# Loading w_in's v columns in pieces of 128 columns, with a lower limit on what is queued ahead of a transfer

## The chip, the core and the metric

The kernel runs on one core of a Trainium2 chip. The metric is the device time of one execution in microseconds, the median of several runs; lower is better.

## The reference

Attention over 8 heads is followed by a gated feed-forward block with a mixing over the sequence. Shapes: batch 4, 8 heads, 768 positions, head size 64; feed-forward width 1024, halved by the gate.

```python
scores = scale * np.matmul(q, k.transpose(0, 1, 3, 2))
keep = is_global | is_local            # first 8 keys, and the last 96 before the query
scores = np.where(keep, scores + bias, -1e9)
a = softmax(scores)
x = np.matmul(a, v)                    # heads laid side by side: 512 columns
...
h = gelu(x @ w_in)                     # w_in: 512 x 1024, 64-bit floats
u, v = h[..., :512], h[..., 512:]
v_n = (v - mean(v)) / sqrt(var(v) + 1e-6) * g_ln
v_s = np.einsum('ts,bsd->btd', w_sg, v_n) + b_sg[None, :, None]
out = x + (u * v_s) @ w_out            # w_out: 512 x 512, 64-bit floats
```

The two halves of `w_in` are called its u columns (0 to 511) and its v columns (512 to 1023).

## The kernel before, in words

**The attention.** It is cut into 48 units: 4 batches, 3 pairs of query blocks (`u`), 4 pairs of heads (`j`). For each unit `load_qk` (L773, issued at L777) brings queries and keys, `load_v` (L780, issued at L784) the values. `score` (matmuls at L794) fills two PSUM banks, `softmax` adds the bias on VectorE (DVE, L825), takes the exponential on ScalarE (ACT, L830), and sums and reciprocals of 4 columns follow (L837 to L843). The first 16 units (`TURNS`) turn the probabilities on TensorE: a diagonal matrix is built (L861), matmuls at L929 turn, and the result is copied out of PSUM (L937 on ACT, L938 on DVE). Later units turn blocks on DVE (L893) and send them through DRAM by four transfers (`far<-tt`, L901) and one back (`pt<-far`, L905). `weigh` (L959) multiplies by the values. For `qk` there are 3 places in SBUF, for `v` 2.

**The feed-forward block.** Every float32 operand is split into a high and a low part, and a product is three matmuls (L466 to L468), accumulated in a PSUM bank: `v_tile` (6 per batch; all four 128-row blocks of the v columns are needed), `u_tile`, `mix_tile` (with `w_sg`) and `out_tile` (with `w_out`), which ends in a store (L595). The block of one batch is woven in between the attention units of the next.

**The weights.** `load_split` (L616) brings a slice of a weight and splits it. A 64-bit weight comes as raw 32-bit words (L628) and is turned into float32 by one ACT and three DVE instructions on a stage (L631, L634, L636, L638); then the high part is written (L641 on ACT or L642 on DVE) and the low part (L643 on POOL or DVE). The slices: `w_v`, four of 128 rows x 512 v columns, in the time of the first four units; `w_u`, eight of 256 u columns; `w_s`, twelve of `w_sg` (32-bit, L624); `w_o`, eight of 256 columns of `w_out`. The stage is a pair of buffers, `raw` and `f`: for `w_v` two places of `z` (`in_z`, L1097), for `w_out` a place of `t` and one of `diag` (`in_t`, L1101), for `w_u` two `View`s of one place of `gt` (`in_gt`, L1108).

**The order.** Nothing of this is run in the order in which it is written down. `op(ways, reads, writes)` enters an operation in a plan (`Plan`, L199), with the engines that could do it and an estimated time on each; reads and writes of a buffer, or of a numbered part of one, give the dependencies. `due` works out when each is needed. `search` (L253) draws 40 plans: for each, three limits and a random shift of every operation's due time, taken from one random sequence in the order of the operations; `order` (L278) plays each plan out, and the one that ends first is written down, engine by engine, by `emit`. All transfers go through SP's queue. In the planner a transfer costs 0.38 us of SP and its bytes at 360 GB/s on a common wire, and SP may not begin one while the wire is booked for over `QUEUED` us ahead:

```python
can = [o for o in sorted(wait[e], key=pe_at.get if e == "PE" else due)
       if o.ready <= t and not (o.dma and wire > t + QUEUED)
       and room(o, e, short)]
```

The first transfer into a buffer needs a free place (`room`). In the program that `emit` writes, SP issues its transfers in the planned order, and each waits by semaphore for its buffer alone. In gaps of TensorE in the first 29 us of the plan, `keep_on` puts dummy matmuls (L415).

Of the kernel before, what the change touches and what calls it, by code (L numbers as in the profile page):

```python
# [14 lines left out]
I32 = mybir.dt.int32  # L15
# [82 lines left out]

LANDS = 1.5

QUEUED = 1.8

TO_QUARTERS, FROM_QUARTERS = 0.095, 0.21

# [1 line left out]
def on_act(n, more=0.0):  # L106

    return "ACT", 0.055 + n / 1200 + more, 0.165 + n / 1200 + more
# [6 lines left out]
def on_dve_sb(n, more=0.0):  # L115

    return "DVE_SB", 0.065 + n / 960 + more, 0.155 + n / 960 + more


def on_pool(n, more=0.0):  # L120
    return "POOL", 0.05 + n / 390 + more, 0.08 + n / 390 + more
# [41 lines left out]
def parts(used):  # L163

    return [(b.buf, b.part) if isinstance(b, View) else b if isinstance(b, tuple) else (b, None)
            for b in used]
# [18 lines left out]
class Now:  # L185
# [5 lines left out]
    def op(self, ways, reads=(), writes=()):  # L191
        for b, _ in parts(writes):
            if b.kind and b.tile is None:
                n = self.next[b.kind] = self.next.get(b.kind, -1) + 1
                b.slot = n % self.places[b.kind]
        ways[0][-1]()


class Plan:  # L199
# [78 lines left out]
    def order(self, start, rules, pace):  # L278
# [40 lines left out]
        def room(o, e, short):  # L319
            need, now = {}, t - (SLACK if e == "SP" else 0.0)  # L320
            for b in firsts(o):
                need[b.kind] = need.get(b.kind, 0) + 1 + b.spare
            lacks = {k for k, n in need.items()
                     if k in short or sum(x is not None and x <= now for x in places[k]) < n}
            short |= lacks
            return not lacks

        while len(done) < len(self.ops):
            went = False
            for e in self.ENGINES:  # L330
                if free[e] > t:
# [3 lines left out]
# [3 lines that stand above are left out]
# [56 lines left out]
            if not went:  # L394
                nexts = [f for f in [wire - QUEUED, *free.values(), *held.values()] if f > t] + [
                    x + more for at in places.values() for x in at if x is not None
# [219 lines left out]
def load_split(nc, plan, stage, t, src, k, cols, part):  # L616


    n, op = cols.stop - cols.start, plan.op
    rows = slice(k * P, (k + 1) * P)  # L620
    wire = lambda words: ("SP", 0.38, P * words * 4 / 360e3)
    raw, f = stage(n)
    if src.dtype != mybir.dt.int64:
        op([wire(n) + (lambda: nc.sync.dma_start(f.ap, src[rows, cols]),)], [], [f])  # L624
    else:
        words = lambda: raw.ap.bitcast(I32).rearrange("p (n w) -> p n w", w=2)
        a = lambda: f.ap.bitcast(I32)
        op([wire(2 * n) + (lambda: nc.sync.dma_start(  # L628
            raw.ap.bitcast(I32), src.bitcast(I32)[rows, 2 * cols.start:2 * cols.stop]),)], [], [raw, f])

        op([on_act(n, 0.07) + (lambda: nc.scalar.mul(  # L631
            f.ap, words()[:, :, 1].bitcast(F32), 2.0 ** -112),)], [raw], [f])

        op([("DVE_SB", 0.07 + n / 1850, 0.15 + n / 1850, lambda: nc.vector.tensor_scalar(  # L634
            a(), a(), 3, None, ALU.logical_shift_left))], [], [f])
        op([on_dve_sb(n, 0.02) + (lambda: nc.vector.scalar_tensor_tensor(  # L636
            a(), words()[:, :, 0], 29, a(), ALU.logical_shift_right, ALU.bitwise_or),)], [raw], [f])
        op([on_dve_sb(n, 0.02) + (lambda: nc.vector.scalar_tensor_tensor(  # L638
            a(), words()[:, :, 1], -0x80000000, a(), ALU.bitwise_and, ALU.bitwise_or),)],
           [raw], [f])  # L640
    op([on_act(n, 0.03) + (lambda: nc.scalar.copy(t[:, 0, k, cols], f.ap),),  # L641
        on_dve_sb(n / 2) + (lambda: nc.vector.tensor_copy(t[:, 0, k, cols], f.ap),)], [f], [(t, part)])  # L642
    lo = lambda eng: eng.tensor_tensor(t[:, 1, k, cols], f.ap, t[:, 0, k, cols].bitcast(F32),  # L643
                                       ALU.subtract)
    op([on_pool(n) + (lambda: lo(nc.gpsimd),), on_dve_sb(n) + (lambda: lo(nc.vector),)],
       [f], [(t, part)])


def local_global_attention_moe(tc, qk_in, v_in, q_t, k_t, v_n, n_gl, w_in, g_ln, w_sg_t, b_sg,
# [506 lines left out]
    def phase(ns, items, prep=()):  # L1156

        total = sum(c for c, _ in items)
        items, prep, done = list(items), list(prep), 0

        def upto(part):
            nonlocal done
            while items and done + items[0][0] / 2 <= part * total:
                c, f = items.pop(0)
                done += c
                f()

        n_prep, todo = len(prep), []
        while len(ns) and (todo[-1][-1] if todo else ns[0] - 1) < ns[-1]:
            todo.append(group(todo[-1][-1] + 1 if todo else ns[0]))  # L1170
        for a, group_ns in enumerate(todo):
            step(group_ns)
            while prep and n_prep - len(prep) < (a + 1) * n_prep / len(todo):
                load_split(nc, plan, *prep.pop(0))
            upto((a + 1) / len(todo))
        upto(2)
# [219 lines left out]
```

## Time and profile before

| | |
|---|---|
| runs | 421.76 us median of 3 (419.79 to 425.49) |
| the profiled execution | 421.83 us, span 420.1 us |
| mean granted TensorE clock | 0.993 |
| busy, share of the span | TensorE (PE) 96%, weight load (PEld) 88%, DVE 77%, ACT 54%, POOL 42% |
| moved by DMA | 68.20 MB, 162 GB/s over the span |

The profile is one execution of the program. Its times are microseconds from the first instruction; the time of the execution also holds what lies around the span. A group of instructions is named by line, engine and operation, with the tile written and the tiles read (`stage<-in_w_in_dram`), a count, and busy time and mean duration. A wait is written `engine line waiting <- what released it: total us, times, longest us`. "issue" as a releaser means that the engine waited for nothing that the profile shows. SPq is the queue of SP, whose entries are transfers begun (a row that joins several has their common stretch, pauses in between included).

### The profile page before, as it was taken

The numbers are of one execution on the slowest core, as the hardware profiler recorded it, in microseconds if no ns is written. First come the engines' busy times: TensorE is split into PE (matmuls) and PEld (weight loads), VectorE is DVE, ScalarE is ACT, GpSimd is POOL, SyncE is SP. The second block draws the span as 40 slices with busy tenths as digits, with TensorE's granted clock in tenths as the row PEclk, the third lists the DMA queues.
The fourth block names the chain that finished last, engine by engine and source line by source line (L and its number), as shares of the span: only waits on it lengthen the run. The fifth ranks groups of instructions, "written<-read, shape, count | busy, mean of one in ns | idle before, by whom it ended". The sixth has DMA issues, their size and how long they took to land.

```text
span 420.1 us, 13632 instructions
## 1 busy us (share of the span) xinstructions
PE 403.7 (96%) x5224; PEld 368.2 (88%) x5224; DVE 323.5 (77%) x1037; ACT 228.2 (54%) x744; POOL 174.6 (42%) x306
## 2 busy tenths in 40 slices
PE   8888989999999999999999999999999999999994
PEld 5766867899998889799999989999999888999994
DVE  6787989999997699995777899885768578754362
ACT  5898889765765765753356556653255343311220
POOL 2234447365686646353554355442553122303100
PEclk9999999989999999999999999999999999999998
DMA  7666575526877778754798785562886521001002
GB/s 246 201 208 166 154 238 153 158 81 173 240 249 255 192 228 238 208 162 114 211 271 227 226 240 141 155 170 54 244 281 172 152 85 39 2 2 48 29 0 81
DMA packets 50040, 68.20 MB, mean 162 GB/s; under 512 B 5809, under 2 KB 33969, under 8 KB 49969
## 3 DMA queue, kind: packets, MB, share of 16 engines
q1 hardware_dynamic: 49968, 67.26, 54.7%
q8 instruction: 43, 0.70, 0.8%
q14 instruction: 29, 0.23, 0.2%
HBM read 48.89 MB, written 18.35 MB: 160 GB/s over the span
## 4 chain that ended last, share of the span: by engine, by line
PE 79%; ACT 6%; DVE 5%; DMA 4%; issue 3%; POOL 1%; SPq 1%; DVEq 0%; POOLq 0%; ACTq 0%
PE mm_ps L466 22%; PE mm_ps L467 21%; PE mm_ps L468 21%; PE s_ps L794 6%; PE av L959 6%; PE tps L929 2%; ACT p L830 2%; DMA pt<-far 2%; DMA qk<-in_qk_in_dram 1%; DMA far<-tt 1%; DVE p L825 1%; DMA v<-in_v_in_dram 1%; ACT stage L631 1%; ACT wsg L641 1%; ACT pt L937 0%
## 5 line engine op out<-in xcount | busy, mean ns | idle before, releaser
L830 ACT ACTIVATE p<-p,pst 128x192 f32<-128x192 f32 (+1 forms) x192 | 84.0, 440 | 36.8 <-DVE pst L825 34.9
L466 PE MATMUL mm_ps<-wsg,z 128*128 128x384 f32 x192 | 65.5, 341 | 0.1
L467 PE MATMUL mm_ps<-wsg,z 128*128 128x384 f32 x192 | 64.9, 338 | 0.0
L468 PE MATMUL mm_ps<-wsg,z 128*128 128x384 f32 x192 | 64.8, 338 | 0.0
L825 DVE CUSTOM_DVE_ANT_0 p<-s_ps,bias 128x192 f32<-128x192 f32 (+1 forms) x192 | 56.5, 337 | 5.1 <-PE s_ps L794 4.9
L851 POOL TENSOR_SCALAR p<-p,pst 128x192 f32<-128x192 f32 (+1 forms) x111 | 50.4, 470 | 15.0 <-DVE pst L843 14.8
L959 PE MATMUL av<-pt,v 64*64 64x128 f32 (+1 forms) x1408 | 47.6, 250 | 1.2 <-DMA pt<-far 1.2
L592 POOL TENSOR_TENSOR o<-o,x 128x384 f32<-128x384 f32 x28 | 28.4, 1013 | 47.5 <-DVE o L589 25.8
L794 PE MATMUL s_ps<-qk 64*64 64x128 f32 (+1 forms) x1408 | 43.1, 249 | 4.1 <-issue 2.5
L794 PEld LDWEIGHTS s_ps<-qk 64*64 64x64 f32 x1408 | 37.1, 134 | 8.9 <-issue 5.7
L466 PE MATMUL mm_ps<-x,win 128*128 128x384 f32 x128 | 44.0, 343 | 0.7 <-ACT pt L937 0.7
L959 PEld LDWEIGHTS av<-pt,v 64*64 64x64 f32 x1408 | 37.2, 134 | 8.2 <-issue 4.9
L468 PE MATMUL mm_ps<-gt,wout 128*128 128x384 f32 x128 | 43.1, 336 | 0.1
L466 PE MATMUL mm_ps<-gt,wout 128*128 128x384 f32 x128 | 43.1, 337 | 0.0
L467 PE MATMUL mm_ps<-gt,wout 128*128 128x384 f32 x128 | 42.9, 335 | 0.0
L468 PE MATMUL mm_ps<-x,win 128*128 128x384 f32 x128 | 42.9, 335 | 0.0
L467 PE MATMUL mm_ps<-x,win 128*128 128x384 f32 x128 | 42.9, 335 | 0.0
L466 PE MATMUL mm_ps<-win,x 128*128 128x512 f32 x96 | 39.6, 412 | 0.0
L500 ACT CAST gt<-y 128x384 fp32r<-128x384 f32 x27 | 13.8, 511 | 46.2 <-DVE y L561 33.4
L467 PE MATMUL mm_ps<-win,x 128*128 128x512 f32 x96 | 37.7, 393 | 0.0
L468 PE MATMUL mm_ps<-win,x 128*128 128x512 f32 x96 | 37.6, 392 | 0.0
L466 PEld LDWEIGHTS mm_ps<-wsg,z 128*128 128x128 f32 x192 | 36.5, 190 | 1.1 <-issue 0.5
(109 smaller groups left out, 905.2 us busy)
## 6 DMA issues: line engine op xcount, KB each, us to landing
qk<-in_qk_in_dram SPq DMA_DIRECT2D x32, 352.0 KB, 3.9
far<-tt SPq DMA_DIRECT2D x96, 96.0 KB, 2.6
pt<-far SPq DMA_DIRECT2D x24, 384.0 KB, 3.9
v<-in_v_in_dram SPq DMA_DIRECT2D x32, 256.0 KB, 3.7
out_dram<-o SPq DMA_DIRECT2D x32, 192.0 KB, 2.7
qk<-in_qk_in_dram SPq DMA_DIRECT2D x16, 288.0 KB, 3.8
v<-in_v_in_dram SPq DMA_DIRECT2D x16, 192.0 KB, 3.6
far<-tt SPq DMA_DIRECT2D x32, 80.0 KB, 2.2
```

Source lines behind the costliest of these rows:

```text
L466: mm(ps.ap, ah, bh, start=(i == 0), stop=False)
L467: mm(ps.ap, ah, bl, start=False, stop=False)
L468: mm(ps.ap, al, bh, start=False, stop=(i == n - 1))
L500: put(out[:, 0, :], src.ap)
L592: lo = lambda eng: eng.tensor_tensor(o.ap, o.ap, xm[:, 1, :].bitcast(F32), ALU.add)
L631: op([on_act(n, 0.07) + (lambda: nc.scalar.mul(f.ap, words()[:, :, 1].bitcast(F32), 2.0 ** -112),)], [raw], [f])
L794: nc.tensor.matmul(s_ps[h][e * HQ:(e + 1) * HQ, i * W + c0:i * W + c0 + n], qk[rows, qc:qc + HQ], qk[rows, QW + k0:QW + k0 + n], start=Tru ...
L825: nc.vector.tensor_tensor_reduce(out=p[:, g, 0:nk], in0=s_ps[h][:, i * W:i * W + nk], in1=bias[:, 2 * j + h, w0:w0 + nk], op0=ALU.add, op1 ...
L830: op([on_act(nk, 0.225) + (lambda p=p, g=g, nk=nk, i=i: nc.scalar.activation(p[:, g, 0:nk], p[:, g, 0:nk], AF.Exp, bias=st[:, 0, i, g:g + ...
L851: op([on_pool_ts(nk, -0.10) + (partial(scaled, lambda o, a, c: nc.gpsimd.tensor_scalar(o, a, c, 1.0, ALU.mult, ALU.mult)),), on_act(nk, 0. ...
L929: nc.tensor.matmul(tps[r][g * HQ:(g + 1) * HQ, a * HQ:(a + 1) * HQ], pc[rows, c:c + HQ], diag[rows, 2 * i + c // W], start=True, stop=True)
L959: nc.tensor.matmul(to, v[rows, vc:vc + D], of, stop=True, skip_group_check=True, **kw)
```

## The change

`QUEUED` goes from 1.8 to 1.5. In `load_split` the transfer of a 64-bit weight's raw words becomes a loop over pieces of 128 columns, each an operation of its own in the plan that writes its own numbered part of `raw` and `f`; the conversion behind it still reads the whole. Where the stage is a `View` there is one piece, as before.

```diff
-QUEUED = 1.8
+PIECE = 128
+
+QUEUED = 1.5
...
         words = lambda: raw.ap.bitcast(I32).rearrange("p (n w) -> p n w", w=2)
         a = lambda: f.ap.bitcast(I32)
-        op([wire(2 * n) + (lambda: nc.sync.dma_start(
-            raw.ap.bitcast(I32), src.bitcast(I32)[rows, 2 * cols.start:2 * cols.stop]),)], [], [raw, f])
+
+        pieces = 1 if isinstance(raw, View) else max(1, n // PIECE)
+        m = 2 * n // pieces
+        for i in range(pieces):
+            op([wire(m) + (lambda i=i: nc.sync.dma_start(
+                raw.ap.bitcast(I32)[:, i * m:(i + 1) * m],
+                src.bitcast(I32)[rows, 2 * cols.start + i * m:2 * cols.start + (i + 1) * m]),)],
+               [], [raw, f] if pieces == 1 else [(raw, i), (f, i)])
 
         op([on_act(n, 0.07) + (lambda: nc.scalar.mul(
             f.ap, words()[:, :, 1].bitcast(F32), 2.0 ** -112),)], [raw], [f])
```

## The prediction

> **What bounds the kernel now.** I read the page first, then a table of stages, then what TensorE waited for, then SP's own queue. The page's head:
>
> ```profile
> span 420.1 us, 13632 instructions
> PE 403.7 (96%) x5224; PEld 368.2 (88%) x5224; DVE 323.5 (77%) x1037; ACT 228.2 (54%) x744; POOL 174.6 (42%) x306
> ```
>
> TensorE (PE) is busy for 96% of the span, so little can be won at all. The table of stages says where the rest lies (its columns: stretch, length, busy time of PE, PEld, DVE, ACT, POOL, granted clock, DMA share, GB/s), and the same table for line 415 alone says how much of the early PE time is the dummy matmuls that the plan puts into gaps:
>
> ```profile
> 0.00:7.00 7.00, 5.68 (x64) 3.21 (x65) 3.78 (x17) 2.31 (x4) 2.41 (x17) 1.00 0.65 186
> 7.00:60.00 53.00, 46.86 (x1373) 37.05 (x1374) 44.11 (x187) 46.06 (x175) 18.70 (x34) 1.00 0.65 201
> 60.00:82.00 22.00, 21.30 (x331) 18.67 (x324) 21.31 (x67) 20.68 (x68) 11.32 (x17) 1.00 0.61 183
> 82.00:86.00 4.00, 2.35 (x93) 1.86 (x88) 3.86 (x14) 2.58 (x8) 1.40 (x3) 1.00 0.02 4
> 86.00:90.00 4.00, 4.00 (x15) 4.00 (x16) 4.00 (x17) 3.15 (x14) 1.95 (x3) 0.57 0.21 72
> 90.00:200.00 110.00, 108.77 (x1263) 99.88 (x1262) 93.46 (x297) 65.88 (x213) 63.09 (x105) 1.00 0.70 202
> 200.00:414.00 214.00, 214.00 (x2114) 203.10 (x2114) 152.42 (x443) 87.50 (x268) 75.70 (x130) 1.00 0.48 136
> ```
>
> ```profile
> 0.00:60.00 60.00, 12.23 (x72) 6.68 (x72) 1.00 0.65 199
> ```
>
> From 200 to 414 us TensorE never stops; from 90 to 200 it lacks 110 - 108.77 = 1.23 us. What the change can move lies before 90 us. Up to 60 us TensorE does 5.68 + 46.86 - 12.23 = 40.3 us of real work, so 19.7 us are filled or empty; but there ACT (46.06 of 53 us) and DVE (44.11 of 53) are nearly full with softmax and weight conversion, and up to 82 us ACT still does 20.68 of 22. ACT's idle time from 7 to 82 us is 6.94 + 1.32 = 8.3 us. That is roughly what a better order could win there, unless it moves work to POOL. Then there is one hole, 82 to 86 us, where PE works 2.35 of 4 us, and behind it 4 us at a granted clock of 0.57.
>
> What does TensorE wait for?
>
> ```profile
> PE s_ps L794 <- issue: 2.5, 2, 1.3
> PE tps L929 <- issue: 2.0, 3, 0.9
> PE s_ps L794 <- ACT pt L937: 1.5, 1, 1.5
> PE s_ps L415 <- DVE bsg L676: 1.2, 1, 1.2
> PE av L959 <- DMA pt<-far: 1.2, 2, 0.8
> ```
>
> For a load from `qk_in`, `v_in` or a weight it does not wait in any of these rows; the one transfer named, `pt<-far`, is a later stage's. The two largest waits, 4.5 us together, are for nothing that the profile shows. For the weights' raw words, the profile of their tile names one DMA among what its readers sat idle for:
>
> ```profile
>   DMA stage<-in_w_out_dram: 2.5, 4
> ```
>
> Those are ACT's four waits for `w_out`, in a stage where ACT does under two thirds (65.88 of 110 us). For `w_in` no wait is named.
>
> **The change part by part.** The sum starts from the profiled execution's 421.83 us (span 420.1 and 1.7 around it), which is the median of the runs, 421.76, to 0.02%.
>
> *Arithmetic.* No conversion, matmul or copy is added or removed: 0 us on each compute engine.
>
> *Pieces, and their issue.* Line 628 becomes a loop. `w_v` has n = 512 and a stage of two `Buf`s: 4 pieces of 128 KB for each of 4 loads, 12 more DMAs. The description names only these, but the test is for `View`, and the stage of `w_out` (`in_t`) has none: its 8 loads with n = 256 become 2 pieces each, 8 more. `w_u` (`in_gt`, views) stays whole, `w_sg` takes the other branch. The prices of an issue on SP, and SP's first 20 us:
>
> ```profile
> L628 SPq DMA_DIRECT2D stage<-in_w_in_dram x12: 327/427/512, 3.1 to 74.0; - x12
> ...
> L628 SPq DMA_DIRECT2D stage<-in_w_out_dram x8: 327/328/516, 76.5 to 104.8; - x8
> ```
>
> ```profile
> 1.18 1.37 SPq L777 DMA_DIRECT2D qk<-in_qk_in_dram  x3
> 2.59 0.43 SPq L784 DMA_DIRECT2D v<-in_v_in_dram  x1
> 3.06 0.44 SPq L628 DMA_DIRECT2D stage<-in_w_in_dram  x1
> 3.55 0.43 SPq L784 DMA_DIRECT2D v<-in_v_in_dram  x1
> 4.02 0.51 SPq L628 DMA_DIRECT2D stage<-in_w_in_dram  x1
> 5.70 1.21 SPq L777 DMA_DIRECT2D qk<-in_qk_in_dram  x2
> 6.96 0.42 SPq L628 DMA_DIRECT2D stage<-in_w_in_dram  x1
> 11.88 3.74 SPq L777 DMA_DIRECT2D qk<-in_qk_in_dram  x2
> ...
> 19.98 0.38 SPq L628 DMA_DIRECT2D stage<-in_w_in_dram  x1
> ```
>
> ```profile
> SPq L628 <- POOL z L504: 8.9, 1, 8.9
> ```
>
> 12 x 0.427 = 5.1 us and 8 x 0.328 = 2.6 us of SP. What hides it: SP stands idle from 7.38 to 11.88, and its queue is mostly waits (8.9 us for one `w_out` load alone). If the cover is gone, that is, if the plan puts all four pieces ahead of a `qk` or `v` load, that load starts 3 x 0.427 = 1.3 us later. I take 0; bounds 0 and 4 x 1.3 = 5.1 us.
>
> *Landing.* The bytes are the same, and the queue is full when the first three loads move; here is the stretch from 3.6 to 13 us, then the issues of the first 32 us, then the page's row of `far<-tt`:
>
> ```profile
> DMA packets 1380, 3.39 MB, mean 361 GB/s; under 512 B 153, under 2 KB 409, under 8 KB 1379
> ```
>
> ```profile
> stage<-in_w_in_dram SPq DMA_DIRECT2D x4, 512.0 KB, 6.5
> qk<-in_qk_in_dram SPq DMA_DIRECT2D x4, 288.0 KB, 4.2
> v<-in_v_in_dram SPq DMA_DIRECT2D x4, 192.0 KB, 4.1
> ```
>
> ```profile
> far<-tt SPq DMA_DIRECT2D x96, 96.0 KB, 2.6
> ```
>
> At 361 GB/s a piece of 128 KB takes 0.36 us, less than the 0.43 us of its issue, and behind a full queue neither shows. The price of a smaller transfer has bounds in two of these rows: 96 KB lands in 2.6 us, 512 KB in 6.5 us, so 9.4 ns per KB on a fixed 1.7 us. If the fixed parts overlap, 0; if each piece paid its own in turn, 3 x 1.7 = 5.1 us on each load. Do they overlap? The four-part transfer `far<-tt` shows it:
>
> ```profile
> 98.60 1.78 SPq L901 DMA_DIRECT2D far<-tt  x4
> ...
> 101.90 0.33 SPq L905 DMA_DIRECT2D pt<-far  x1
> ```
>
> The reader of all four could be issued 3.30 us after the first began, not 4 x 2.6 = 10.4 us. They overlap; I take 0. The Trainium skill speaks against the change here: its page "DMA: Bandwidth & Descriptors", in "Rules for kernel authors", asks for transfers of 1 MiB and more and for many small ones to be made one. By that rule each load would be some us dearer, which is the fourth rival below; the row of the four parts says that transfers in flight together do not add up.
>
> *Less ahead in the queues.* `QUEUED` stands only in the planner: at 1.5 it puts off a transfer in the plan by up to 0.3 us. SP gets no instruction from it, so what is really ahead in the queues is not capped. By 4.53 us SP had begun 3 x 288 + 2 x 192 + 2 x 512 = 2272 KB, which at 361 GB/s is 6.4 us of transfers, whatever 1.8 says. What reaches the chip is the order of SP's queue: a `qk` that becomes ready can stand behind one piece instead of behind the whole load, up to 3 x 0.36 = 1.1 us sooner. As no compute engine is shown waiting for these loads, the gain is 0; bounds -1.1 and 0.
>
> *The plan drawn again.* 20 more operations mean other random shifts for all 40 drawn plans, so every engine's order may change, everywhere. This is the largest unknown and has no direction that I can read. Its price goes by the holes: the one at 82 to 86 us costs 4 - 2.35 = 1.65 us of idleness and 4 x 0.43 = 1.7 us of clock, 3.4 us together. The Trainium skill, "TensorE: Matmul & The Clock Gate", asks to avoid idle gaps of over some 3 us between bursts of matmuls; by that a hole of 1.65 us should cost no clock, and this one would be worth 1.65. The trace disagrees: the clock halves behind it. A wait "for nothing" costs 0.9 to 1.3 us. I take 0; bounds: one hole and two such waits less, 3.4 + 2.2 = -5.6, or two holes more, +6.8.
>
> Sum: 421.8 + 0 = 421.8 us.
>
> **The rivals.**
>
> 1. *The new order is tighter*: the hole at 82 us closes and one wait of 1.2 us goes: 421.8 - 3.4 - 1.2 = 417.2 us. For it: ACT and DVE have 8.3 us of idle time that a finer interleaving may use. Against: they are over 85% busy with a chain of softmax steps, and this hole comes after ACT's `pt` copy, not after a load.
>
> 2. *SP is held by the pieces* (slower): all four pieces of each `w_v` load stand ahead of the next `qk` or `v`, and those land 1.3 us later, four times; ACT, full, starts each softmax that much later: 421.8 + 5.1 = 426.9 us. It decides from the point where `qk` or `v` becomes what TensorE waits for (above 0 us in its rows). Against: SP's idle stretches, and a planner that orders by due time and can now change over between pieces.
>
> 3. *More holes*: the redrawn order opens two more holes like that at 82 us before 90 us: 421.8 + 6.8 = 428.6 us. It decides from a stretch of 4 us in which TensorE works under 60%. Three of them would pass 2%.
>
> 4. *Small transfers add up*: the four `w_v` loads land in these times (least, middle, most), and the last is first read at 26.00:
>
> ```profile
> DMA to landing us min/median/max: 5.3/6.5/7.0
> ```
>
> ```profile
> 26.00 0.69 ACT L631 ACTIVATE stage<-stage 128x512 f32<-128x512 f32 x1
> ```
>
> It is issued at 19.98, so it lands at 25.3 at the earliest and has at most 0.7 us of slack; 5.1 us more on it delays the first `v` tile by at least 4.4 us: 426.2 us. Against: the row of `far<-tt`.
>
> 5. *It does nothing that it says*: the queue on the chip stays as deep, and the order is the old one: 421.8 us too, told from the forecast only by an unchanged order of SP's queue.
>
> **How the numbers follow.** Chances: forecast (another order, same time) 0.52, tighter 0.20, SP held 0.10, more holes 0.07, small transfers 0.04, nothing done 0.07. The forecast's own range is 418 to 425.5: a hole's 3.4 us either way, and the runs themselves spread from 419.79 to 425.49. The range for 8 in 10 reaches down past the tighter case to 416 and up to 428, past rivals 2 and 4 and just short of 3. A change of 2%, 8.4 us, is about what a measurement of this kernel can tell from no change. Faster than 413.4 would need the hole, both largest waits and more to go at once: 0.05. Slower than 430.2 needs three holes, or rivals 2 and 3 together: 0.06. Between them 0.89.
>
> **What would show it.** Right: 16 loads of 128 KB from `in_w_in_dram`, 16 from `in_w_out_dram`, 8 of 256 KB from `in_w_in_dram`; the real PE work before 60 us within 2 us of 40.3; PE at 214.0 of 214 us in the late stretch; no row in which TensorE waits for `qk` or `v`. Wrong: a row of PE or PEld waiting over 1 us for one of these loads (rival 2), ACT's raw-word step at line 631 waiting for `in_w_in_dram` (rival 4), other low-clock stretches (rival 3), or a time under 416 us with ACT's idle time before 82 us cut well below 8.3 us, which would mean that the order of loads did set the pace.

## The result and the profile after

| | before | after |
|---|---|---|
| median of 20 runs | 422.22 us (419.79 to 425.95) | 426.48 us (423.20 to 430.38) |
| the profiled execution | 421.83 us, span 420.1 | 428.83 us, span 427.2 |

The ratio of after to before is 1.0094, with a 95% interval of 1.0065 to 1.0122: slower by 0.9%, 4.0 us of 421.8. That is less than the 2% mark, but clear of 1. The ratio leaves out three executions of after that ran in a slower state, so it is not the quotient of the two medians. The profiled execution of after is 2.3 us longer than the median of its runs, so its stages are read for where time goes, not for the last microsecond.

The page of after, head and transfers:

```profile
span 427.2 us, 13689 instructions
PE 405.3 (95%) x5228; PEld 368.3 (86%) x5228; DVE 315.3 (74%) x1021; ACT 225.4 (53%) x737; POOL 194.4 (45%) x329
...
DMA packets 52919, 68.20 MB, mean 160 GB/s; under 512 B 6128, under 2 KB 38384, under 8 KB 52848
```

The issues of after by line:

```profile
stage<-in_w_in_dram SPq DMA_DIRECT2D x16, 128.0 KB, 4.1
stage<-in_w_in_dram SPq DMA_DIRECT2D x8, 256.0 KB, 4.3
stage<-in_w_out_dram SPq DMA_DIRECT2D x16, 128.0 KB, 3.7
```

The change did what it says, and did it to `w_out` as well. The megabytes are the same. Another thing in the head was not written into the code by anyone: DVE has 16 instructions fewer and POOL 23 more. Each operation may go to one of several engines, and the new plan dealt them out in another way. The stages of after, with the boundaries used for before:

```profile
0.00:7.00 7.00, 5.66 (x63) 3.20 (x64) 3.76 (x17) 2.28 (x4) 2.42 (x17) 1.00 0.64 195
7.00:60.00 53.00, 46.21 (x1355) 36.96 (x1355) 43.11 (x184) 46.38 (x177) 20.66 (x35) 1.00 0.66 203
60.00:82.00 22.00, 21.09 (x338) 18.73 (x331) 21.17 (x67) 19.61 (x65) 12.21 (x16) 1.00 0.57 177
82.00:86.00 4.00, 3.59 (x34) 3.24 (x33) 4.00 (x14) 2.54 (x6) 1.04 (x2) 1.00 0.02 5
86.00:90.00 4.00, 4.00 (x76) 3.44 (x78) 4.00 (x15) 3.64 (x13) 3.21 (x6) 1.00 0.65 205
90.00:200.00 110.00, 104.00 (x1250) 93.55 (x1241) 87.61 (x287) 63.87 (x214) 69.25 (x115) 0.98 0.69 197
200.00:414.00 214.00, 214.00 (x2113) 202.74 (x2112) 147.59 (x438) 86.54 (x263) 85.61 (x142) 1.00 0.47 135
```

Two things changed places. The hole at 82 to 86 us is gone, and with it the low clock behind it: TensorE works 3.59 of 4 us instead of 2.35, and the clock from 86 to 90 is 1.00 instead of 0.57. But from 90 to 200 us it now lacks 110 - 104.00 = 6.0 us, where it lacked 1.2, at a mean clock of 0.98. The stretch in steps of 4 us shows where:

```profile
104.00:108.00 4.00, 3.43 (x19) 2.83 (x17) 2.79 (x7) 1.77 (x7) 2.82 (x5) 1.00 0.84 301
108.00:112.00 4.00, 2.71 (x71) 2.58 (x72) 3.19 (x10) 1.67 (x4) 1.74 (x3) 1.00 0.88 280
...
128.00:132.00 4.00, 1.88 (x7) 0.99 (x5) 1.13 (x3) 0.72 (x3) 1.84 (x5) 0.88 0.89 278
132.00:136.00 4.00, 4.00 (x72) 3.70 (x72) 2.76 (x11) 1.08 (x4) 1.15 (x2) 0.69 0.98 344
```

And these are TensorE's waits in after from 98 to 140 us:

```profile
PE mm_ps L468 <- ACT wsg L649: 2.0, 1, 2.0
PE av L967 <- DMA pt<-far: 1.9, 1, 1.9
PE s_ps L802 <- DVE o L591: 0.5, 1, 0.5
PE mm_ps L470 <- POOL wout L651: 0.2, 1, 0.2
```

None of them is for a load that the change cut into pieces. The two large ones are for a slice of `w_sg` that is split late, and for probabilities on their way through DRAM; the last, of 0.2 us, is for the splitting of a slice of `w_out`. So is it the transfers, or only the order?

### The profile page after: what moved, and what is told of

Its sections match the earlier page's. It is cut to its first block, busy times and chain, and to the rows that moved or that the text cites. A ratio compares the mean times of both kernels' runs of the same rounds, so it can differ in the third digit from the quotient of the medians.

```text
span 427.2 us, 13689 instructions
## 1 busy us (share of the span) xinstructions
PE 405.3 (95%) x5228; PEld 368.3 (86%) x5228; DVE 315.3 (74%) x1021; ACT 225.4 (53%) x737; POOL 194.4 (45%) x329
## 4 chain that ended last, share of the span: by engine, by line
PE 68%; DMA 9%; DVE 9%; ACT 4%; issue 4%; POOL 3%; SPq 2%; DVEq 0%; POOLq 0%; ACTq 0%
PE mm_ps L468 18%; PE mm_ps L470 17%; PE mm_ps L469 17%; PE av L967 6%; PE s_ps L802 6%; DMA far<-tt 5%; PE tps L937 2%; DMA v<-in_v_in_dram 2%; SPq L909 2%; ACT p L838 2%; DVE p L833 2%; DMA stage<-in_w_out_dram 1%; DVE tt L901 1%; PE tps L417 1%; DMA qk<-in_qk_in_dram 1%
## 5 line engine op out<-in xcount | busy, mean ns | idle before, releaser
L859 POOL TENSOR_SCALAR p<-p,pst 128x192 f32<-128x192 f32 (+1 forms) x122 | 54.6, 463 | 16.4 <-DVE pst L851 16.4
L901 DVE STREAM_TRANSPOSE tt<-p 128x384 f32<-128x384 f32 (+1 forms) x64 | 33.4, 544 | 8.6 <-DMA far<-tt 5.5
```

Of the source, the lines that this page charges most:

```text
L859: op([on_pool_ts(nk, -0.10) + (partial(scaled, lambda o, a, c: nc.gpsimd.tensor_scalar(o, a, c, 1.0, ALU.mult, ALU.mult)),), on_act(nk, 0. ...
L901: nc.vector.transpose(out, src.rearrange("p g (b j) -> p g b j", j=QB))
```

## The experiments

The theories: (1) the transfers in pieces cost nothing, and what costs is that the plan was drawn anew; in its sharper form (1a) the order of the kernel before is a good draw, which any redrawing loses. Against it: (2) smaller transfers, or SP held by them, cost the time; (3) the lower `QUEUED` makes worse orders; (4) the pieces as operations of the plan make worse orders; (5) both settings together do, whatever the draw. The time of one kernel differs from round to round of runs (the kernel before took 419.98, 420.52 and 420.65 us in the three rounds below), so each ratio is to the kernel before in the same round.

### Pieces without a new order, and a new order without pieces

The first kernel keeps the operation of before, so that the plan is the same, and only issues more transfers in its place:

```diff
-        op([wire(2 * n) + (lambda: nc.sync.dma_start(
-            raw.ap.bitcast(I32), src.bitcast(I32)[rows, 2 * cols.start:2 * cols.stop]),)], [], [raw, f])
+        at = lambda i, p: slice(2 * n // p * i, 2 * n // p * (i + 1)); bring = lambda p: [nc.sync.dma_start(
+            raw.ap.bitcast(I32)[:, at(i, p)], src.bitcast(I32)[rows, 2 * cols.start:2 * cols.stop][:, at(i, p)])
+            for i in range(p)]
+        op([wire(2 * n) + (lambda: bring(1 if isinstance(raw, View) else n // 128),)], [], [raw, f])
```

> The order of every engine is that of the kernel before, instruction by instruction; only each raw-word load of w_in's v columns is issued as 4 transfers and each of w_out as 2, in the same place of SP's queue. Theory 1 (the order drawn anew is what costs, transfers in pieces cost nothing): the time of the kernel before, 422 us, within 1.5 us. Theory 2 (smaller transfers, or SP held by them, cost the time): 425 to 428 us, with TensorE waiting for loads or SP's queue late in the first 25 us and from 76 to 110 us.

Measured: 420.57 us, 1.0016 times the kernel before, interval 0.9991 to 1.0041. The pieces cost 0.7 us of 420, and by the interval between -0.4 and 1.7. SP's queue in this kernel:

```profile
2.59 0.43 SPq L784 DMA_DIRECT2D v<-in_v_in_dram  x1
3.06 1.86 SPq L628 DMA_DIRECT2D stage<-in_w_in_dram  x4
4.96 0.43 SPq L784 DMA_DIRECT2D v<-in_v_in_dram  x1
5.67 2.09 SPq L628 DMA_DIRECT2D stage<-in_w_in_dram  x4
7.87 0.84 SPq L777 DMA_DIRECT2D qk<-in_qk_in_dram  x2
8.76 1.85 SPq L628 DMA_DIRECT2D stage<-in_w_in_dram  x4
```

Here rival 2 of the prediction is put to the test by itself, and more harshly than it was drawn: all pieces stand ahead of the next loads, the second `v` is begun at 4.96 instead of 3.55 us, and the `qk` pair at 7.87 instead of 5.70. It did not matter: the time shows nothing of the up to 2.2 us that those loads lost.

The second kernel keeps the plan of after, and lets the first piece's operation bring the whole load:

```diff
             op([wire(m) + (lambda i=i: nc.sync.dma_start(
-                raw.ap.bitcast(I32)[:, i * m:(i + 1) * m],
-                src.bitcast(I32)[rows, 2 * cols.start + i * m:2 * cols.start + (i + 1) * m]),)],
+                raw.ap.bitcast(I32), src.bitcast(I32)[rows, 2 * cols.start:2 * cols.stop])
+                if i == 0 else None,)],
```

> The order of every engine is that of the changed kernel; the first piece's operation brings the whole load and the others issue nothing, so the transfers are whole again. Theory 1: the time of the changed kernel, 426.5 us, within 1.5 us, with the holes between 104 and 132 us still there. Theory 2: back to 422 us.

Measured: 424.85 us, 1.0091 times before, interval 1.0064 to 1.0119, where the changed kernel has 1.0094. (As a time it is 0.15 us below the 425.0 to 428.0 that was expected; the kernel before was faster in this round too.) With whole transfers and the new order the loss is all there. The two kernels settle theory 2 against theory 1: the order carries the loss, the transfers carry none that can be measured.

### One setting at a time

In the kernel before, and in the changed one:

```diff
-QUEUED = 1.8
+QUEUED = 1.5
```

> QUEUED is 1.5, no pieces. Theory 1: another order from the same random shifts, any time from 418 to 430 us; it need not lie near the changed kernel. Theory 3 (the lower limit on what is queued ahead makes the planned order worse in the stretch with the many transfers, 100 to 140 us): 425 us or more, with holes of 4 us or more in all from 100 to 140 us.

```diff
-QUEUED = 1.5
+QUEUED = 1.8
```

> Pieces as in the changed kernel, QUEUED back at 1.8. Theory 1: another order, any time from 418 to 430 us. Theory 3: 422 us or less, without the holes from 100 to 140 us. Theory 4 (more operations of the pieces in the plan, with the second piece of w_out standing ahead of other transfers, make the order worse): 425 us or more, with holes from 100 to 140 us again.

Measured: `QUEUED` alone 424.83 us, 1.0114 (1.0085 to 1.0142); pieces alone 424.31 us, 1.0096 (1.0071 to 1.0121). Each alone loses what both together lose, so the losses are not a sum of two parts: every new order seems to cost about 1%. TensorE's idle time lies at different places in them; the stretches 60 to 100 and 100 to 140 us of the kernel before, then of `QUEUED` alone, then of the pieces alone:

```profile
60.00:100.00 40.00, 37.65 (x486) 34.54 (x477) 38.59 (x118) 30.87 (x99) 22.09 (x30) 0.96 0.45 138
100.00:140.00 40.00, 39.14 (x485) 36.11 (x487) 34.12 (x107) 25.98 (x87) 26.96 (x41) 1.00 0.81 240
```

```profile
60.00:100.00 40.00, 35.56 (x516) 32.35 (x509) 37.51 (x125) 31.89 (x102) 22.32 (x31) 1.00 0.44 136
100.00:140.00 40.00, 39.40 (x511) 35.78 (x510) 34.49 (x114) 25.07 (x87) 27.66 (x47) 1.00 0.80 242
```

```profile
60.00:100.00 40.00, 37.11 (x521) 33.59 (x513) 38.91 (x122) 31.78 (x100) 27.08 (x37) 1.00 0.43 138
100.00:140.00 40.00, 38.30 (x504) 34.78 (x503) 33.66 (x112) 25.16 (x90) 29.42 (x50) 1.00 0.85 254
```

`QUEUED` alone has its 4.4 us of idle time before 100 us and almost none from 100 to 140. Theory 3 needed holes of 4 us there and falls by their place, though 424.83 us nearly is the 425 that it asked for; and with `QUEUED` back at 1.8 the time did not return to 422 us, as it also asked. Theory 4 wanted 425 us and holes there too; pieces alone took 424.31 us and have 1.7 us there and 2.9 us before 100, so it is not borne out, and that `QUEUED` alone loses as much needs no theory of the pieces. The rows place the idle time, but they do not add up to the 1%: the kernel before itself has 2.35 us of idle time and 1.6 us of lost clock from 60 to 100 us.

### Other draws

If the order before is a good draw, the old settings must lose as well when only the random sequence changes (its seed, the number that it starts from, becomes 2, 3 or 4):

```diff
-        rnd = random.Random(1)
+        rnd = random.Random(2)
```

> The kernel before with the plans drawn from another random sequence (seed 2 in place of 1), nothing else. Theory 1a (the order before was a good draw, and any redrawing costs about what the changed kernel lost): 1.005 to 1.015 times the kernel before, that is 422 to 426 us beside 420. Theory 5 (the orders that come of the changed settings are worse than those of the old ones, whatever the draw): 0.995 to 1.005.

> The kernel before with seed 3. As for seed 2: theory 1a 1.005 to 1.015 times the kernel before, theory 5 0.995 to 1.005.

> The changed kernel with seed 2. Theory 1a: another draw from the same spread as the others, 0.995 to 1.015 times the kernel before. Theory 5: 1.008 or more, as with seed 1.

> The changed kernel with seed 3. Theory 1a (the order before was a good draw; the settings make no difference over many draws): 1.000 to 1.020 times the kernel before, like the other redrawn orders. A further theory, 6 (the changed settings give better orders on the whole, which one good draw of the old ones hides): below the old settings with the same seed, 1.021, by 0.005 or more, as it was with seed 2 (1.007 beside 1.013).

> The kernel before with seed 4. Theory 1a: 1.005 to 1.020 times the kernel before. If it comes out at 0.995 to 1.003, the order before was no special draw, and theory 1a is weaker.

Two more kernels draw 120 plans instead of 40; the first 40 are the same ones, and a later one is taken because it ends earlier in the planner's reckoning.

```diff
-PLANS, DRAWN, STRETCH, REACH = 40, 40, 40.0, 180.0
+PLANS, DRAWN, STRETCH, REACH = 120, 120, 40.0, 180.0
```

> The kernel before with 120 plans drawn in place of 40, the first 40 of them the same; among the other 80 one ends earlier in the planner's reckoning and is written down. If the planner's ranking holds on the chip at this level, 0.990 to 0.999 times the kernel before. If it does not (theory 1a in its strict form: below about 1% a draw's place on the chip is chance), 1.003 to 1.020, like any other redrawn order.

> The changed kernel with 120 plans drawn, the first 40 the same; here too a later one ends earlier in the planner's reckoning. If the planner's ranking holds on the chip, faster than the changed kernel, 0.995 to 1.006 times the kernel before; if not, 1.003 to 1.020.

Measured, as ratios to the kernel before:

| drawn from | old settings | the change |
|---|---|---|
| seed 1, 40 plans | 1 (the kernel before) | 1.0094 (1.0065 to 1.0122) |
| seed 2 | 1.0129 (1.0071 to 1.0187) | 1.0068 (1.0035 to 1.0101) |
| seed 3 | 1.0210 (1.0141 to 1.0278) | 1.0120 (1.0058 to 1.0182) |
| seed 4 | 1.0123 (1.0078 to 1.0168) | |
| seed 1, 120 plans | 1.0042 (1.0003 to 1.0081) | 1.0147 (1.0085 to 1.0208) |

With the two kernels of the section above these are eleven orders. The one of the kernel before is the fastest of them, and the ten others lie from 1.0042 to 1.0210, with a mean of 1.0114. The changed kernel at 1.0094 is an ordinary member. The means of the columns are 1.0101 and 1.0107, and the old settings lose as much as the change when they are redrawn: theory 5 falls. Theory 6 (the changed settings give better orders on the whole) got what it expected with seeds 2 and 3, where the change is ahead by 0.0061 and 0.0090, but with the two draws of seed 1 the change is behind by 0.0094 and 0.0105; it is not borne out, and not excluded. Theory 1a stands, with one miss: it gave the old settings with seed 3 at most 1.015, and they came out at 1.0210. With 120 plans the planner found orders that end earlier by its own reckoning, and neither is faster on the chip than the one taken from 40. So in these two cases its ranking does not hold on the chip; no version was found that beats the kernel before.

### Is one hole worth its size?

The prediction priced orders by holes. One of the largest waits of the changed kernel, TensorE's 2.0 us for ACT's cast of a `w_sg` slice, can be taken away without changing the order:

```diff
-    op([on_act(n, 0.03) + (lambda: nc.scalar.copy(t[:, 0, k, cols], f.ap),),
-        on_dve_sb(n / 2) + (lambda: nc.vector.tensor_copy(t[:, 0, k, cols], f.ap),)], [f], [(t, part)])
-    lo = lambda eng: eng.tensor_tensor(t[:, 1, k, cols], f.ap, t[:, 0, k, cols].bitcast(F32),
-                                       ALU.subtract)
+    frm = lambda: plan.bsg[:, 0:n] if src.dtype == F32 and k == 5 and cols.start else f.ap
+    op([on_act(n, 0.03) + (lambda: nc.scalar.copy(t[:, 0, k, cols], frm()),),
+        on_dve_sb(n / 2) + (lambda: nc.vector.tensor_copy(t[:, 0, k, cols], frm()),)], [f], [(t, part)])
+    lo = lambda eng: eng.tensor_tensor(t[:, 1, k, cols], frm(), t[:, 0, k, cols].bitcast(F32), ALU.subtract)
...
-    plan.on = on
+    plan.on, plan.bsg = on, w.bsg
```

> The changed kernel in its own order; the last slice of w_sg (128 rows x 384 columns) is split from the tile of b_sg, which has long been there, instead of from its transfer, which is still made, so this slice's values are others. It takes away one wait: ACT's cast of that slice, for which TensorE stands still 2.0 us near 130 us and behind which the granted clock is low. If that hole is worth its idleness and its clock (2.0 + about 1.7 us), the time falls by 3 to 4 us to 1.000 to 1.003 times the kernel before. If what waits there only moves on to the next late buffer, it falls by under 1 us and stays at 1.007 or more.

Measured: 426.49 us, 1.0139 (1.0089 to 1.0189). The expected gain of 3 to 4 us did not come. TensorE's row at that place in the kernel with the same order and the wait (new order, whole transfers; its profiled execution took 423.75 us, that of the kernel without the wait 423.49), and then TensorE's rows without it:

```profile
128.46 0.44 PE L468 MATMUL mm_ps<-wsg,z 128*128 128x384 f32 x1 [1.97 <-ACT wsg L649]
```

```profile
128.12 0.68 PE L967 MATMUL av<-pt,v 64*64 64x128 f32 x24 [0.94 <-DMA pt<-far]
...
134.52 0.68 PE L967 MATMUL av<-pt,v 64*64 64x128 f32 x24 [1.19 <-ACT p L857]
```

The brackets hold the idle time before a group and what ended it. The 1.97 us are gone, and 0.94 + 1.19 = 2.13 us have come: first for probabilities from DRAM, then for ACT's scaling of the next ones. The stretch as a whole, from 100 to 140 us, has TensorE at 36.89 us with the wait and a clock of 0.96, and at 35.79 us without it and a clock of 1.00:

```profile
100.00:140.00 40.00, 36.89 (x449) 33.09 (x439) 32.88 (x110) 24.89 (x90) 26.00 (x42) 0.96 0.83 262
```

```profile
100.00:140.00 40.00, 35.79 (x441) 32.11 (x440) 32.74 (x111) 25.52 (x92) 27.70 (x45) 1.00 0.84 259
```

Idleness and lost clock together are 3.1 + 1.6 = 4.7 us in the one and 4.2 us in the other. This reads as if the stretch were limited by the chain from scores through ACT, DVE and DRAM back to TensorE, and not by the one buffer that happened to come last; that only one wait gave way to others is shown, the limit itself is not.

## Why the prediction was right or wrong

The time lay in the range for 8 in 10, and most steps held; the likeliest case, no change, was not what happened. The 426.5 us lie 1 us past the forecast's own 418 to 425.5. The wider range holds them because it was drawn up to 428 to take in rivals 2 and 4, neither of which happened, so that part is luck. The prediction took 2% for the least change that can be told from none; with 20 runs of each kernel the interval is 0.3% either way.

- **Arithmetic, 0 us**: held. TensorE's late stretch is 214.0 of 214 us again, and the real work before 60 us is 39.6 us (51.88 busy less 12.27 of dummies) beside 40.3.
- **Pieces and their issue, 0 us, bounds to 5.1**: held, 0.7 us (-0.4 to 1.7) by the kernel with pieces in the old order. An issue cost near what it was put at (1.86 us for four, 0.465 each, beside 0.427). The reason was right too: no engine was waiting for `w_in`'s loads. That `w_out` is cut up as well, which the title does not say, was read rightly from the code. There ACT does wait, and longer with pieces (2.5 us before, 4.0 with pieces in the old order; in the new order 3.7 with whole loads, 7.1 with pieces), but ACT has room there (63.87 of 110 us busy after), and the time shows none of it.
- **Landing, 0 us**: held. A piece lands in a middle of 4.1 us beside 6.5 for the whole load, four in flight together, and no row of after has an engine waiting for `in_w_in_dram`. The rule of the Trainium skill against many small transfers ("DMA: Bandwidth & Descriptors", "Rules for kernel authors") does not reach the time here: in the full queue the rate was 349 GB/s with pieces beside 361 without, the kernel with pieces in the old order is not slower, and rival 4 falls. The straight line of the prediction would have given 2.9 us for 128 KB; it was 4.1 in a queue that was busy for 99% of that stretch, with no effect on the end.
- **Less ahead in the queues, 0 us**: nothing speaks for a direct effect; its own kernel differs from the one before by its order alone, and loses like any other order.
- **The plan drawn again, 0 us without direction, -5.6 to +6.8**: this is the step that failed, by +4.0 us of 421.8, inside its bounds. To put it at 0, the order before had to be a typical draw. It is the fastest of eleven, so a redraw had a direction, and a typical one loses 1.1%. A single profile does not show where in the spread its order stands. TensorE's 108.77 us in the stretch from 90 to 200 us are second of the eleven (nine others have from 104.0 to 108.3 there), but the highest, the 109.4 of `QUEUED` alone, belongs to an order that loses 1.1% all the same.
- **The rivals**: the hole at 82 us closed, as the tighter case wanted, and the time rose. *More holes* was nearest in kind, with its time 2.1 us too long (428.6) and its place wrong: they opened at 104 to 132 us, not before 90. The price of a hole as idleness plus clock was wrong as a saving: one hole closed gave nothing. Its clock part is not even fixed: with the pieces in the old order the same hole, 1.55 us beside 1.53, has a clock of 1.00 behind it (rows in the last section). *SP is held* came within half a microsecond of the time (426.9) and is refuted: the kernel with all pieces ahead of `qk` and `v` is not slower, and without the pieces the loss stays. Its sign, TensorE waiting for a `v` load, does stand in after, but with 0.4 us in one place. *Small transfers add up* came within 0.3 us (426.2) and is refuted by the same two kernels. *It does nothing that it says* falls by the issues, 16 of 128 KB for `w_in`. One figure in the first rival is not both engines': the 8.3 us of idle time are ACT's, DVE has 9.6.

What stays open: which property of an order decides its time on the chip, since the planner's own end does not; how the order before came to be the fastest, by selection or by luck (one of eleven orders must be, and by luck alone it is this one once in eleven); and whether the change would pay on the mean of many draws, for which four draws with intervals of up to 0.7% either way are too few.

## What to carry to other kernels

Where a kernel's order comes out of a search with random draws, an edit that adds an operation or moves a limit also redraws the order, and an order that was kept because it was fast is likely to lose by that. Separate the two: hold the order and make only the physical edit, then hold the edit's order and undo it physically. And before a wait is priced as a gain, ask what is late next; here a wait of 2.0 us gave way to two of 2.1 us together, and the drop of the clock that is seen behind a hole in one execution can be missing in another.

## What the runs showed of the hardware

Loads of 512 KB in four of 128 KB, issued back to back from SP, went with a slightly lower rate in the full queue, which the kernel's time does not show. From 3.6 to 13 us the queue of the changed kernel moved 349 GB/s, that of the same order with whole transfers 361:

```profile
DMA packets 2537, 3.28 MB, mean 349 GB/s; under 512 B 279, under 2 KB 1944, under 8 KB 2536
...
q1 hardware_dynamic: 2536, 3.27, 99.4%
```

```profile
DMA packets 1381, 3.40 MB, mean 361 GB/s; under 512 B 153, under 2 KB 409, under 8 KB 1380
...
q1 hardware_dynamic: 1380, 3.38, 97.0%
```

In the order before it was 334 GB/s with pieces and 361 without. These are two pairs of single executions with a nearly equal mix of loads; both go the same way, and the size is rough. The engines' time was nearly full in each (97.0 to 100.2%), with over 1.7 times the packets where the loads were in pieces.

The granted clock can fall behind idle time of TensorE well under 3 us, and the length of the gap alone does not decide whether it falls. In the kernel before it was 0.57 from 86 to 90 us, behind a gap of 1.53 us. In the kernel with the pieces in the old order TensorE has the same gap, 1.55 us long, and the clock stays:

```profile
82.00:86.00 4.00, 2.84 (x46) 2.60 (x47) 3.97 (x16) 3.69 (x12) 2.07 (x2) 1.00 0.01 2
86.00:90.00 4.00, 4.00 (x25) 4.00 (x24) 4.00 (x13) 2.30 (x9) 2.40 (x3) 1.00 0.22 70
```

In the new order there is a gap of 1.32 us near 31 us, among shorter ones. With whole transfers, where it ends at 31.61 us and TensorE works 1.65 of the 4 us from 30 to 34, the clock is low behind it:

```profile
34.00:38.00 4.00, 4.00 (x65) 3.29 (x55) 2.36 (x11) 3.27 (x16) 2.74 (x6) 0.57 0.51 128
```

In the changed kernel, where it ends at 32.45 us and TensorE works 1.81 and 2.51 us in the two stretches of 4 us from 28 to 36, the clock stays:

```profile
36.00:40.00 4.00, 4.00 (x80) 3.23 (x84) 1.92 (x12) 3.96 (x15) 2.10 (x6) 1.00 0.54 172
```

The longest gap of `QUEUED` alone, 3.36 us, left the clock at 1.00, as its row for 60 to 100 us has it, further up:

```profile
76.54 0.81 PE L929 MATMUL tps<-diag,p 64*64 64x64 f32 x40 [3.36 <-POOL diag L861]
```

So what a hole costs in clock differs between executions of nearly the same work, and what decides it is open here. The 3 us that the Trainium skill gives for a harmful gap ("TensorE: Matmul & The Clock Gate", "Why this matters for your kernels") are not a safe bound by these rows: the clock fell where the longest gaps were 1.32 and 1.53 us, and held behind one of 3.36.
